# A Fourier token-mixing kernel: the inverse transform's first stage in four quarter tiles of the array, its second in whole-array products

## The chip, the cores and the metric

The kernel runs on one core of a Trainium2 chip. The metric is the time of one execution on the device, in microseconds (us); less is better. In what follows PE is TensorE (the matrix unit, 128 rows by 128 columns), DVE is VectorE, ACT is ScalarE, POOL is GpSimd and SP is SyncE, whose queue issues every DMA of this kernel. PSUM is the memory that PE writes its products into, in banks of 512 float32 a partition.

## The reference, cut to what matters

```python
def _attn_ref(x, filt_r, filt_i):                 # x: 8 x 3136 x 256
    X = np.fft.rfft(x, axis=1)                    # along the 3136 tokens
    Y = X * (filt_r + 1j * filt_i)[None, :, :]
    return np.fft.irfft(Y, n=x.shape[1], axis=1)

def _moe_ref(x, w_ch1, w_ch2):                    # x: what _attn_ref gave
    mixed = np.real(np.fft.fft(np.fft.fft(x, axis=1), axis=2))
    u = x + mixed
    un = (u - mean(u)) / sqrt(var(u) + 1e-6)      # over the 256 channels
    return u + np.maximum(un @ w_ch1, 0.0) @ w_ch2
```

A filter in the frequency domain for each of 8 batches, then a Fourier mixing over tokens and channels (the token part of it is at hand already: it is the filtered spectrum), a normalisation, and a two-layer perceptron with 1024 hidden units.

## The kernel before, in words

All float32 data that goes into PE is split into two float16 parts, high and low, and a product is the sum of three: high by high, high by low, low by high.

**Per batch, the way out** (`there`, lines 598-602). `forward1` (372-405; for batch 0 `first_forward1`, 331-370) loads x in seven tiles of 112 partitions, finds the largest value (`absmax`, on DVE), splits x, multiplies by the 112 x 112 matrix `s1` (line 400: three matmuls of 512 columns for each of 14 pieces), splits the result into `st` on ACT and DVE, and stores it to a scratch array `d1` in DRAM. `forward2` (413-541) loads `d1` back transposed in seven chunks `at` (line 425), and in each chunk does for both halves of the channels: 16 matmuls of 56 columns with the `s2` matrices (`spectrum`, lines 449-450), the filter on DVE and POOL (455-464), the split into `y16`, and a transpose into `z` (for batch 0 on PE, `flip`; for the others by a DMA, line 480). Two chunks later comes the **first inverse stage**, `inverse1` (509-520): two steps a chunk, each of them six matmuls 112 x 112 by 256 columns (lines 514-516: two residues `j`, three products each) into one PSUM bank, the split of the bank into `bt` by ACT (518) and DVE (519), and a store to the scratch array `d2` (520). `fold` (482-507) prepares sums and differences `eo` for the channel mixing.

**Per batch, the way home** (`back`, 604). `inverse2` (543-594) loads `d2` back in seven pieces (554), and in 14 steps does the **second inverse stage**: four matmuls of 512 columns (line 577), in two column tiles of 64 columns of the array: `h` picks the half of the array and of the 128 output partitions, and the two terms of a half, `i`, are accumulated; the high and the low part of the data lie on alternating partitions, so that one pass takes both. ACT scales the bank into `ys` (584), and after each second step four DMAs (five in the first) store `ys` to a scratch array `dy` (560).

**For all tokens** (lines 608-988): groups of 256 slots. `fetch` loads them from `dy`, `prepare` mixes channels (646), normalises and splits into `ut`; `first_product` (six matmuls of 512 columns, line 770) and `second_product` (12 matmuls of 256 columns, line 799) are the perceptron, eight times for each of 49 groups. Their evictions are lines 779 (ACT), 780 and 808 (DVE).

**What sets the order.** The main loop (976-993) goes over the 8 x 49 perceptron pieces. With each, it lets the way out of the next batch go on by some of its steps (`advance`: a batch has `STEPS` = 63 steps, 24 for `forward1`, 4 of pause, 35 for `forward2`: five a chunk, namely `spectrum` twice, `inverse1` twice and `fold`), and the way home by one (`give`: `BACK` = 17 steps a batch). `folds` says at which step a fold would overwrite the ring `eo`; `weigh` places the loading and splitting of the weights at numbered steps during batch 0. Tiles wait for a free buffer of their pool; the PSUM pool `ps_f` of four banks serves both forward stages, both inverse stages and the channel mixing. The order of the instructions on each engine is made by the tile framework from a simulated timeline, by the order of the program, and `after(...)` pins some DMAs and products behind others. All DMAs go through SP's queue in order: one that waits for its data holds up all that stand behind it.

Of the kernel before, what the change touches and what calls it, by code (L numbers as in the profile page):

```python
# [9 lines left out]
F32 = mybir.dt.float32  # L10
# [4 lines left out]
ALU = mybir.AluOpType  # L15
# [23 lines left out]
STEPS = FIRST + PAUSE + 7 * 5  # L39
# [6 lines left out]
LOAD_AT = (19, 20, 21, 22, 50, 50, 54, 54)  # L46
LOAD_AFTER = (("d1", 10), ("d1", 11), ("d1", 12), ("d1", 13), ("bt", 3), ("bt", 3), ("bt", 4), ("bt", 4))
LOAD_IN = ("ut", "ut", "ys", "ys", "big", "big", "big", "big")
WIDEN_AT = (58, 59, 60, 61, 62, 63, 64, 65)
BOUND_AT = (62, 66)  # L50
SPLIT_AT = (63, 115)
# [29 lines left out]
def residue(h, jp):  # L81
    return jp if h == 0 else (28 if jp == 0 else 56 - jp)


# [5 lines left out]

def constants():
    k = slot_freqs()
    n1 = np.arange(112)
    n2 = np.arange(28)
    s1 = np.zeros((112, 56, 2))
    s2 = np.zeros((56, 2, 28, 2, 28))
    for U in range(56):
        j, s = divmod(U, 2)
        th2 = 2 * np.pi * ((n2[:, None] * k[U][None]) % N) / N
        if U == 0:  # L100
            s1[:, 0, 0] = 1
            s1[:, 0, 1] = np.where(n1 % 2, -1, 1)
            lo = n2 < 14
            s2[0, 0, :, 0, :] = np.cos(th2) * lo
            s2[0, 0, :, 1, :] = -np.sin(th2) * lo
            s2[0, 1, :, 0, :] = np.cos(th2) * ~lo
            s2[0, 1, :, 1, :] = -np.sin(th2) * ~lo
            s2[0, 0, :, 1, 0] = np.where(n2 % 2, -1, 1)
        else:
            k1 = 28 if U == 1 else (j if s == 0 else 56 - j)  # L110
            th = 2 * np.pi * ((n1 * k1) % 112) / 112
            s1[:, U, 0] = np.cos(th)
            s1[:, U, 1] = -np.sin(th)
            s2[U, 0, :, 0] = np.cos(th2)
            s2[U, 1, :, 0] = np.sin(th2)
            s2[U, 0, :, 1] = -np.sin(th2)
            s2[U, 1, :, 1] = np.cos(th2)

    p = channel_order()[:129]
# [7 lines left out]

    ncls = np.array([residue(h, jp) for h in range(2) for jp in range(28)])
    i1 = np.zeros((28, 2, 2, 28, 56, 2))
    for j in range(28):  # L130
        for s in range(2):
            for q in range(28):
                U = 2 * j + s
                kk = k[U, q]
                for ri in range(2):
                    if U == 0 and q == 0:
                        con = [(0, 1.0)] if ri == 0 else [(N // 2, 1.0)]
                    elif ri == 0:
                        con = [(kk, 1.0), ((N - kk) % N, 1.0)]
                    else:  # L140
                        con = [(kk, 1j), ((N - kk) % N, -1j)]
                    for tgt, ro in [(j, None)] if j else [(0, 0), (28, 1)]:
                        for kq, cf in con:
                            if kq % 56 != tgt:
                                continue
                            v = cf * np.exp(2j * np.pi * ((ncls * kq) % N) / N) / 32
                            if ro is None:
                                i1[j, ri, s, q, :, 0] += v.real
                                i1[j, ri, s, q, :, 1] += v.imag
                            else:  # L150
                                i1[j, ri, s, q, :, ro] += v.real

    tok = slot_tokens()
    i2 = np.zeros((2, 2, 2, 28, 64))
    j = np.arange(28)
    for jp in range(2):
        for kind in range(2):
            for s in range(2):
                h = s if kind == 0 or jp == 0 else 1 - s
                for q in range(28):  # L160
                    n = tok[kind, 2 * jp + s, q]
# [886 lines left out]
```

## Time and profile before

| | |
|---|---|
| median of three runs | 1534.46 us (1533.2 to 1537.94) |
| the profiled execution: from its first to its last instruction | 1534.0 us |
| busy: PE | 1398.7 us (91%), 11331 matmuls |
| busy: DVE / ACT / POOL | 1092.8 us (71%) / 771.3 us (50%) / 539.9 us (35%) |
| granted TensorE clock, mean | 0.955 |
| DMA | 268.98 MB, 429491 packets, the 16 engines busy for 72.5% of the span |

A row of an instruction group in the profile names the line, the engine and the operation, what is written and read, the shape (partitions x elements), the count, the busy time and the mean duration of one, and the idle time of the engine ahead of it with what ended it. A row of the timeline gives start and length of a run of equal instructions. Matmuls are pipelined: the length of one (385 ns for 512 columns) is longer than the distance to the next, so the cost of a matmul is read from the distances between starts.

### The profile page before, as it was taken

Reading aid. Unit: us, or ns where it says so; the run is one execution under the profiler, and the core shown is the slowest. Engines: PE = TensorE matmul, PEld = TensorE weight load, DVE = VectorE, ACT = ScalarE, POOL = GpSimd, SP = SyncE. Lnnn points to the kernel's source line nnn. Section 1 sums busy time; section 2 is a strip of 40 time slices with the busy share of each in tenths; the row PEclk is TensorE's granted clock in tenths of the full one; section 3 lists DMA queues with packets and bytes.
Section 4 is the critical chain, followed back from the end, with each engine's and each line's share of the span. In section 5 each row is a group of like instructions: output and inputs, shape, how many; then the busy total and the mean of one; then the engine's idle time right before and its main releaser. Section 6 shows DMA issues by size and latency. Waiting matters only on the chain.

```text
span 1534.0 us, 30300 instructions
## 1 busy us (share of the span) xinstructions
PE 1398.7 (91%) x11331; PEld 934.1 (61%) x11331; DVE 1092.8 (71%) x2388; ACT 771.3 (50%) x1426; POOL 539.9 (35%) x682
## 2 busy tenths in 40 slices
PE   5454899787999999999999999899999999999998
PEld 1432567454665677566765677566665667666666
DVE  5576878586967887687758877688767877565562
ACT  4466545354545464474544654374644655443341
POOL 3652049205810195006720284016620284110110
PEclk8675999998999999999999999999999999999999
DMA  8868478959985797859986796859876896644320
GB/s 263 218 205 219 101 163 176 219 157 206 203 216 146 175 227 174 208 152 214 192 192 161 192 231 159 211 146 220 183 189 158 195 237 144 166 107 110 95 55 29
DMA packets 429491, 268.98 MB, mean 175 GB/s; under 512 B 218624, under 2 KB 395824, under 8 KB 429344
## 3 DMA queue, kind: packets, MB, share of 16 engines
q1 hardware_dynamic: 429344, 267.05, 72.5%
q8 instruction: 89, 1.46, 0.4%
q14 instruction: 58, 0.48, 0.1%
HBM read 113.36 MB, written 102.76 MB: 141 GB/s over the span
## 4 chain that ended last, share of the span: by engine, by line
PE 67%; DMA 11%; DVE 7%; issue 3%; POOL 3%; ACT 2%; SPq 1%; DVEq 0%; POOLq 0%; ACTq 0%
PE h L770 26%; PE acc L799 26%; DMA x<-x 3%; PE s L400 3%; PE y L577 3%; DMA at<-d 2%; PE mix L646 2%; DVE y L656 2%; PE i L514 1%; DMA b<-d 1%; PE i L516 1%; PE i L515 1%; PE s L449 1%; DVE mx L267 1%; PE s L450 1%
## 5 line engine op out<-in xcount | busy, mean ns | idle before, releaser
L770 PE MATMUL h<-ut,w1s 128*128 128x512 f16 x2352 | 590.8, 385 | 24.6 <-DVE h L780 20.5
L799 PE MATMUL acc<-w2s,h 128*128 128x256 f16 x4704 | 599.9, 274 | 1.3 <-DVE h L780 1.3
L799 PEld LDWEIGHTS <-h 128*128 128x128 f16 x4704 | 456.4, 98 | 146.8 <-issue 13.6
L779 ACT ACTIVATE h<-h 128x512 f16<-128x512 f32 x392 | 233.1, 595 | 411.9 <-PE h L770 404.6
L780 DVE SCALAR_TENSOR_TENSOR h<-h,h 128x512 f16<-128x512 f32 x392 | 267.6, 683 | 200.3 <-ACT h L779 199.3
L741 POOL TENSOR_TENSOR u<-un,u 128x512 f16<-128x512 f32 x94 | 107.8, 1163 | 758.0 <-ACT u L739 745.6
L770 PEld LDWEIGHTS <-w1s 128*128 128x128 f16 x2352 | 223.8, 99 | 236.7 <-issue 48.1
L656 DVE SCALAR_TENSOR_TENSOR y<-mix,alpha,y 128x508 f32<-128x508 f32 (+1 forms) x368 | 156.0, 474 | 8.2 <-PE mix L646 6.9
L736 ACT ACTIVATE un<-y,sb 128x256 f32<-128x256 f32 x196 | 101.8, 589 | 44.0 <-DVE sb L729 38.8
L469 POOL TENSOR_TENSOR y<-yt,y 128x448 f16<-128x448 f32 x105 | 108.4, 1036 | 16.5 <-ACT y L468 16.2
L584 ACT ACTIVATE ys<-y,alpha 128x512 f32<-128x512 f32 x112 | 76.1, 686 | 71.4 <-PE y L577 71.0
L519 DVE TENSOR_TENSOR bt<-i,bt 112x512 f16<-112x512 f32 x112 | 75.7, 682 | 49.1 <-ACT bt L518 47.4
L267 DVE TENSOR_REDUCE mx<-x 112x1 f32<-112x1024 f32 x56 | 67.7, 1214 | 52.0 <-DMA x<-x 52.0
L463 POOL TENSOR_TENSOR yt<-yt,t 128x224 f32<-128x224 f32 x112 | 73.9, 660 | 81.9 <-DVE t L459 53.6
L455 DVE SCALAR_TENSOR_TENSOR yt<-s,pF,ft 128x448 f32<-128x448 f32 x112 | 75.3, 675 | 37.7 <-PE s L450 34.9
L449 PE MATMUL s<-s,at 112*128 112x56 f16 x896 | 62.7, 191 | 32.6 <-DMA at<-d 28.1
L400 PE MATMUL s<-x,s 112*112 112x512 f16 x294 | 87.3, 388 | 3.9 <-ACT x L394 1.9
L577 PE MATMUL y<-b,i 112*64 112x512 f16 (+1 forms) x480 | 74.1, 396 | 18.1 <-DMA b<-d 17.9
L518 ACT CAST bt<-i 112x512 f16<-112x512 f32 x112 | 64.9, 585 | 49.9 <-PE i L516 43.7
L808 DVE SCALAR_TENSOR_TENSOR y<-acc,beta,y 128x512 f32<-128x512 f32 x98 | 71.2, 742 | 25.7 <-PE acc L799 25.5
L468 ACT CAST y<-yt 128x448 f16<-128x448 f32 x112 | 62.6, 564 | 38.6 <-POOL yt L464 35.6
L449 PEld LDWEIGHTS <-at 112*128 112x128 f16 x896 | 55.8, 98 | 42.6 <-DMA at<-d 36.0
(133 smaller groups left out, 1663.4 us busy)
## 6 DMA issues: line engine op xcount, KB each, us to landing
x<-x SPq DMA_DIRECT2D x56, 448.0 KB
d<-ast SPq DMA_DIRECT2D x112, 224.0 KB
at<-d SPq DMA_DIRECT2D x56, 448.0 KB
d<-bt SPq DMA_DIRECT2D x112, 224.0 KB
b<-d SPq DMA_DIRECT2D x56, 448.0 KB
out<-y SPq DMA_DIRECT2D x98, 256.0 KB
y<-dy SPq DMA_DIRECT2D x92, 256.0 KB
dy<-ys SPq DMA_DIRECT2D x208, 112.0 KB
```

The lines of the kernel that those rows point to most:

```text
L267: nc.vector.tensor_reduce(dst, src, axis=axis, op=ALU.max, apply_absolute_value=True)
L400: nc.tensor.matmul(p, s1[:, hs], x16[:, hx], start=i == 0, stop=i == 2)
L449: nc.tensor.matmul(o, w, s2[:, U, 0].rearrange("p (r k) -> p r k", r=2), start=True, stop=False)
L469: last = half(b, hf == 1).tensor_tensor(ylo, ytv, yhi, op=ALU.subtract)
L577: nc.tensor.matmul(p[64 * h : 64 * h + 64, js], i2[:, t, h, i], bt[:, o + js.start : o + js.stop, h], start=i == 0, stop=i == 1,)
L656: nc.vector.scalar_tensor_tensor(out, p, al, y, op0=ALU.mult, op1=ALU.add)
L736: nc.scalar.activation(un[:m, k], y[:m, t, k], AF.Identity, bias=sb[:m, i, 1:2], scale=sb[:m, i, 3:4])
L741: marks["u16", g] = low.tensor_tensor(u16[:m, :, :, 1], unv, u16[:m, :, :, 0], op=ALU.subtract).ins
L770: marks["pe"] = nc.tensor.matmul(p[:, c0 : c0 + n].rearrange("p (t k q) -> p t k q", k=2, q=m), w1s[:, d, hw, 128 * f : 128 * f + 128], ut ...
L779: nc.scalar.activation(h[:, 0, :nt], p[:, :nt], AF.Relu)
L780: marks["h"] = nc.vector.scalar_tensor_tensor(h[:, 1, :nt], p[:, :nt], 0.0, h[:, 0, :nt], op0=ALU.max, op1=ALU.subtract).ins
L799: nc.tensor.matmul(acc[:m, k], h[:, hh, c0 : c0 + m], w2s[:, f, hw], start=f == 0 and k == 0 and i == 0, stop=f == 7 and k == 1 and i == 2,)
```

## The change

1. **x in slot order.** The host lays the tokens of x out in the order in which the kernel numbers its slots. The first forward matrix `s1` now forms an even and an odd part of each of two token halves: it has 128 output columns (two parts, 56 used of 64 each), and a second version of it for the first token class (`cls`). `st` and `d1` have 128 partitions in place of 112. `s2` is kept for each part `P`; chunk 0 gets extra products with a small matrix `s2x`.
2. **First inverse stage.** `inverse1` is one step a chunk. Both PSUM banks of the chunk are taken at once. The 64 x 64 quarters of the array work on their own products: the row half `h` picks the residue pair and the bank, the column half `P` the part. Six matmuls of 256 columns for each quarter, 24 a chunk (30 in chunk 0, with `i1x`), are issued in turns over the four quarters (`run`), all but the first at high priority. Each bank is scaled and split into `bt` by ACT and DVE as before, and stored by two DMAs in place of one.
3. **Second inverse stage.** Three matmuls of 512 columns over the whole array (`dense`) in place of four in two column tiles; the high and low parts lie side by side in a row of `d2`. Two stores to `dy` for each second step in place of four.
4. **Steps.** `STEPS` is 56: four steps a chunk in `forward2`. The numbered steps for weights and folds are moved along. `at` is loaded by two DMAs, one for each part, in place of one. `bt` and `st` share six buffers in place of four.

The diff, cut to its core:

```diff
-STEPS = FIRST + PAUSE + 7 * 5
+STEPS = FIRST + PAUSE + 7 * 4
...
-    s1 = cp.tile([112, 2, 112], F16, name="s1")
+    s1 = cp.tile([112, 2, 2, 128], F16, name="s1")
+    s2x = cp.tile([112, 2, 2, 56], F16, name="s2x")
-    i1 = cp.tile([112, 28, 2, 112], F16, name="i1")
-    i2 = cp.tile([112, 2, 2, 2, 64], F16, name="i2")
+    i1 = cp.tile([128, 14, 2, 2, 64], F16, name="i1")
+    i1x = cp.tile([64, 2, 2, 64], F16, name="i1x")
+    i2 = cp.tile([112, 2, 2, 128], F16, name="i2")
...
+    def run(todo):
+        for i in range(max(len(m) for m in todo)):
+            for n, m in enumerate(todo):
+                if i < len(m):
+                    o, w, x, start, stop = m[i]
+                    with tc.high_priority() if i + n else nullcontext():
+                        nc.tensor.matmul(o, w, x, start=start, stop=stop)
+
+    def dense(p, w, xs, special):
+        last = None
+        for sl, cls in ((slice(0, 1), 1), (slice(1, 2), 0)) if special else ((slice(0, 2), 0),):
+            terms = [(v, x) for v, x in zip(w(cls), xs)]
+            for i, (v, x) in enumerate(terms):
+                last = nc.tensor.matmul(p[:, sl], v, x[:, sl], start=i == 0, stop=i == len(terms) - 1)
+        return last
...
-            for i, (hs, hx) in enumerate(((0, 0), (0, 1), (1, 0))):
-                nc.tensor.matmul(p, s1[:, hs], x16[:, hx], start=i == 0, stop=i == 2)
-            st = fp.tile([112, 2, 2, 256], F16, tag="ast", name=f"ast_{b}_{q}", bufs=4)
+            dense(p, split_of(s1), [x16[:, i] for i in (0, 1, 0)], q == 0)
+            st = fp.tile([128, 2, 2, 256], F16, tag="ast", name=f"ast_{b}_{q}", bufs=6)
...
-                last = nc.sync.dma_start(ats[ch], d1v[:, 8 * ch : 8 * ch + 8])
+                for P in range(2):
+                    last = nc.sync.dma_start(ats[ch][:, P], d1v[:, P, 4 * ch : 4 * ch + 4])
...
+            for j in range(4):
+                for P in range(2):
+                    o = p[:, P, 56 * j : 56 * j + 56]
+                    of = [(at[:, P, j, 128 * hf : 128 * hf + 128], s2[:, 4 * ch + j, P])]
+                    if ch + j == 0:
+                        of.append((at[:, 1 - P, j, 128 * hf : 128 * hf + 128], s2x[:, 1 - P]))
+                    ms = [(w, m[:, i]) for w, m in of for i in range(2)]
+                    for i, (w, m) in enumerate(ms):
+                        with order if j + P + i == 0 else nullcontext():
+                            nc.tensor.matmul(o, w, m, start=i == 0, stop=i == len(ms) - 1)
...
-        def inverse1(ch, h):
-            z = zs[ch][:112].rearrange("p (j l) c -> p j l c", l=2)[:, 2 * h : 2 * h + 2]
-            j = 4 * ch + 2 * h
-            p = bank(f"i1_{b}_{ch}_{h}")[:112].rearrange("p (j c) -> p j c", j=2)
-            for i in range(2):
-                nc.tensor.matmul(p[:, i], i1[:, j + i, 0], z[:, i, 0], start=True, stop=False)
-                nc.tensor.matmul(p[:, i], i1[:, j + i, 0], z[:, i, 1], start=False, stop=False)
-                nc.tensor.matmul(p[:, i], i1[:, j + i, 1], z[:, i, 0], start=False, stop=True)
-            bt = fp.tile([112, 2, 2, 256], F16, tag="ast", name=f"bt_{b}_{ch}_{h}", bufs=4)
-            nc.scalar.copy(bt[:, :, 0], p)
-            marks["low"] = nc.vector.tensor_tensor(bt[:, :, 1], p, bt[:, :, 0], op=ALU.subtract).ins
-            marks["bt", ch] = nc.sync.dma_start(d2[:, j : j + 2], bt).ins
+        def inverse1(ch):
+            z = zs[ch].rearrange("p (r l i) c -> p r l i c", r=2, l=2)
+            p = [bank(f"i1_{b}_{ch}_{h}").rearrange("p (i c) -> p i c", i=2) for h in range(2)]
+            todo = []
+            for h in range(2):
+                for P in range(2):
+                    rows, mine = slice(64 * h, 64 * h + 56), []
+                    for i in range(2):
+                        ws = i1[rows, 2 * ch + i, P]
+                        ms = [(ws[:, m], z[rows, P, l, i]) for m, l in ((0, 0), (0, 1), (1, 0))]
+                        if ch + h + i == 0:
+                            ms += [(i1x[rows, 1 - P, m], z[rows, 1 - P, l, i]) for m, l in ((0, 0), (0, 1), (1, 0))]
+                        o = p[h][64 * P : 64 * P + 64, i]
+                        mine += [(o, w, x, n == 0, n == len(ms) - 1) for n, (w, x) in enumerate(ms)]
+                    todo.append(mine)
+            run(todo)
+            for h in range(2):
+                bt = fp.tile([128, 2, 2, 256], F16, tag="ast", name=f"bt_{b}_{ch}_{h}", bufs=6)
+                nc.scalar.activation(bt[:, :, 0], p[h], AF.Copy, scale=1.0 / 32)
+                marks["low"] = nc.vector.scalar_tensor_tensor(
+                    bt[:, :, 1], p[h], 1.0 / 32, bt[:, :, 0], op0=ALU.mult, op1=ALU.subtract
+                ).ins
+                for P in range(2):
+                    marks["bt", ch] = nc.sync.dma_start(
+                        d2[:, P, :, 4 * ch + 2 * h : 4 * ch + 2 * h + 2].rearrange("m r j l x -> m r (j l x)"),
+                        bt[64 * P : 64 * P + 56].rearrange("p i l x -> p (i l x)"),
+                    ).ins
...
-                for js, t in parts:
-                    for i in range(2):
-                        for h in range(2):
-                            nc.tensor.matmul(
-                                p[64 * h : 64 * h + 64, js],
-                                i2[:, t, h, i],
-                                bt[:, o + js.start : o + js.stop, h],
-                                start=i == 0,
-                                stop=i == 1,
-                            )
-            nc.scalar.activation(ys[:, o : o + 2], p, AF.Copy, scale=al[:, 2:3])
+                dense(p, split_of(i2), [bt[:, ms, i] for i in (0, 1, 0)], c == 0)
+            nc.scalar.activation(ys[:, ms], p, AF.Copy, scale=al[:, 2:3])
+            if c % 2:
+                for k in range(2):
+                    marks["sp"] = marks["dy"] = nc.sync.dma_start(
+                        dy[k, 224 * (c // 2) : 224 * (c // 2) + 224].rearrange("(j q) c -> q j c", j=4), ys[64 * k : 64 * k + 56]
+                    ).ins
...
-        d1 = dp.tile([112, 28, 2, 256], F16, tag="d1", name=f"d1_{b}")
-        d2s[b] = dp.tile([112, 28, 2, 256], F16, tag="d2", name=f"d2_{b}")
+        d1 = dp.tile([128, 28, 2, 256], F16, tag="d1", name=f"d1_{b}")
+        d2s[b] = dp.tile([28, 2, 2, 28, 2, 256], F16, tag="d2", name=f"d2_{b}")
...
-        "x": c(x.reshape(nb, 112, 28, C)[..., perm]),
+        "x": tokens(x[..., perm]),
```

More of the change, by code (lines that the diff above doesn't have):

```diff
@@ new lines, in hi_lo @@
+def hi_lo(a, axis):
+    return np.stack(split16(a), axis=axis)
+def constants():
+    a1, a2 = transforms()
+    inv = a1.transpose(0, 2, 1, 4, 3).reshape(2, 2, 2, 28, 2, 56).swapaxes(3, 4).reshape(2, 2, 2, 56, 56)
+    q = np.arange(28)
+    at = q // 4 * 4 + q % 2 * 2 + q % 4 // 2
+    inv = inv.reshape(2, 2, 2, 2, 28, 56)[..., at, :].reshape(2, 2, 2, 56, 56) * 4096 / N
+    sign = np.array([[1.0, 1.0], [1.0, -1.0]])
+    s1 = np.zeros((2, 56, 2, 2, 64))
+    i2 = np.zeros((2, 56, 2, 2, 64))
+    for cls in range(2):
+        s1[:, :, cls, :, :56] = np.einsum("kq,qpio->kipo", sign, a1[cls])
+        i2[:, :, cls, :, :56] = np.einsum("kp,qpio->qiko", sign, inv[cls])
+    s1, i2 = (m.reshape(112, 2, 128) for m in (s1, i2))
+    s2 = a2[:, [0, 1], [0, 1]]
+    rows = [np.stack([v, v], axis=-2) for v in (s2, a2[0, [0, 1], [1, 0]])]
+    packed = []
+    for v in rows:
+        h, l = split16(v)
+        l[..., 1, :] = 0
+        v = np.stack([h, l], axis=-2).reshape(v.shape[:-3] + (112, 2, 56))
+        packed.append(np.ascontiguousarray(np.moveaxis(v, -3, 0)))
+    w = np.ones((28, 2, 56))
+    w[0, :, 0] = 0.5
+    back = (a2 * w[:, None, :, None]).transpose(0, 2, 1, 4, 3).reshape(28, 2, 2, 56, 2, 28)
+    back = np.pad(back.swapaxes(4, 5).reshape(28, 2, 2, 56, 56), ((0, 0),) * 4 + ((0, 8),))
+    i1 = np.zeros((2, 64, 14, 2, 64))
+    i1[:, :56] = back[:, [0, 1], [0, 1]].reshape(14, 2, 2, 56, 64).transpose(1, 3, 0, 2, 4)
+    i1x = np.zeros((64, 2, 64))
+    i1x[:56] = back[0, [0, 1], [1, 0]].transpose(1, 0, 2)
@@ L126, in constants @@
     cmix[0, 0, 256:] = 1
[L128 to L151, printed above, removed]
@@ L279, in _program @@
     mixed = [0]
[L280 removed]
+    y16s = [cp.tile([128, 2, 2, 4, 64], F16, name=f"y16_{h}") for h in range(4)]
     for t in y16s:
[L282 removed]
+        nc.gpsimd.memset(t[..., 56:], 0.0)
     sxs, alphas, dys, esps = {}, {}, {}, {}
@@ L430, in load @@
                         load_i1(ch)
+                        if ch == 0:
+                            nc.sync.dma_start(s2x, a["c_s2x"])
+                            nc.sync.dma_start(i1x, a["c_i1x"])
                         if ch == 6:
@@ L914, in give @@
             come[0] += 1
-    folds = {FIRST + PAUSE + (4, 9, 14, 19, 24, 29, 34)[ch]: 224 * ch + 224 for ch in range(7)}
+    folds = {FIRST + PAUSE + (4, 8, 12, 16, 20, 24, 27)[ch]: 224 * ch + 224 for ch in range(7)}
     def need(slot):
```

192 lines of the change are left out of this document (85 added, 107 removed).

## The prediction, made before the changed kernel was built or run

> **What bounds the kernel now.** I read the page first, then the stretches, then single visits of PE to the two stages on the timeline, and last the waits. The page:
>
> ```profile
> span 1534.0 us, 30300 instructions
> PE 1398.7 (91%) x11331; PEld 934.1 (61%) x11331; DVE 1092.8 (71%) x2388; ACT 771.3 (50%) x1426; POOL 539.9 (35%) x682
> PE 67%; DMA 11%; DVE 7%; issue 3%; POOL 3%; ACT 2%; SPq 1%; DVEq 0%; POOLq 0%; ACTq 0%
> ```
>
> PE is the busiest engine and holds two thirds of the chain that ends last. A share over the whole span mixes stages, so the stretches follow (columns: stretch, its length, busy time of PE, weight loads, DVE, ACT, POOL, granted clock, DMA share, GB/s):
>
> ```profile
> 0.00:50.00 50.00, 21.75 (x52) 8.38 (x53) 22.10 (x47) 15.70 (x31) 14.81 (x28) 0.77 0.88 266
> 340.00:370.00 30.00, 18.46 (x165) 9.93 (x165) 21.60 (x57) 15.46 (x30) 11.05 (x14) 0.72 0.86 205
> 370.00:1400.00 1030.00, 1005.22 (x8291) 675.32 (x8289) 766.03 (x1684) 537.56 (x997) 387.16 (x489) 0.99 0.78 184
> 540.00:548.00 8.00, 7.64 (x60) 5.34 (x57) 5.73 (x13) 4.99 (x10) 8.00 (x10) 1.00 1.03 249
> ```
>
> From 370 to 1400 us PE is busy for 1005 of 1030 us at nearly the full clock. There, PE time that is taken away should come off the span. The start is another matter: PE works less than half of the first 50 us, and DMA is at 0.88. Between 340 and 370 us stands one hole, which comes back below. So the question is how many PE slots the change frees in batches 1 to 7, and what new waits it makes.
>
> **The first inverse stage.** Seven chunks in each of batches 1 to 7 are 49 visits. One step of such a visit, six matmuls, and what follows it:
>
> ```profile
> 559.24 0.27 PE L514 MATMUL i<-z,i 112*112 112x256 f16 x1
> ...
> 559.79 0.27 PE L516 MATMUL i<-z,i 112*112 112x256 f16 x1
> 559.90 0.38 PE L770 MATMUL h<-ut,w1s 128*128 128x512 f16 x1
> ```
>
> Six matmuls take 559.90 - 559.24 = 0.66 us, 0.109 us each; a chunk has two steps, 1.31 us. The change has 24 matmuls in four quarters: if four run together, six rounds. Nothing in this trace uses quarter tiles. The nearest rows are a visit to the second inverse stage, which uses two column tiles. Timeline of PE, the second pair of the same visit (from a narrower window), and the weight loads:
>
> ```profile
> 630.51 1.47 PE L799 MATMUL acc<-w2s,h 128*128 128x256 f16 x12
> 631.91 0.62 PE L577 MATMUL y<-b,i 112*64 112x512 f16 x4
> 632.47 1.47 PE L770 MATMUL h<-ut,w1s 128*128 128x512 f16 x6
> 633.77 1.47 PE L799 MATMUL acc<-w2s,h 128*128 128x256 f16 x12
> 635.09 0.38 PE L770 MATMUL h<-ut,w1s 128*128 128x512 f16 x1
> ```
>
> ```profile
> 632.15 0.38 PE L577 MATMUL y<-b,i 112*64 112x512 f16 x2
> ```
>
> ```profile
> 631.91 0.14 PEld L577 LDWEIGHTS <-i 112*64 112x64 f16 x4 [0.21 <-issue]
> 632.47 0.11 PEld L770 LDWEIGHTS <-w1s 128*128 128x128 f16 x2 [0.41 <-issue]
> ```
>
> Reading: 12 matmuls of L799 take 635.09 - 633.77 = 1.32 us when a whole-array product follows, but 631.91 - 630.51 = 1.40 when the tiled visit follows: going in costs 0.08 to 0.09 us. Six matmuls of L770 take 1.30 us, so one of 512 columns takes 0.217. The first pair starts at 631.91, the second at 632.15: two matmuls of 512 columns really ran together, with a lag of 0.023 us. The next product starts 0.32 after the second pair: going out costs 0.10. So a visit pays 0.20 us for changing the array's layout and back (its loads wait too, 0.21 and 0.41 us).
>
> For four quarters a round is at best 0.109 us (one matmul of 256 columns) and with the lag of the pair 0.132. I take 0.12, between two near ends. A visit is then 6 x 0.12 + 0.20 = 0.92 us in place of 1.31, a gain of 0.39; 42 visits gain 16.4 us. Chunk 0 has three extra products in two quarters, nine rounds: 1.28 us, a gain of 0.03, seven times 0.2. Sum: **-16.6 us** (ends -20.1 and -12.8).
>
> Whether weights load while another product runs decides this. In the rows above all four loads of the visit, two of them for the second pair, start within 0.14 us of the first pair, 0.10 us ahead of the second pair's start, and all use the same 112 rows. Against this speaks a sentence in the Trainium skill, "TensorE: Matmul & The Clock Gate", section "Part 3: Packing small matmuls — row/col tiling": a weight load overlaps running matmuls "only when row_grp differs". By it, each round's loads would wait for the round before; this trace disagrees for column tiles. It has a rival of its own below.
>
> **The second inverse stage.** Before: 0.09 + 0.56 = 0.65 us (the rows above). After: three whole-array matmuls, 3 x 0.217 = 0.65 us, with no change of layout. **0 us**; two column tiles plus the change of layout cost what a third product costs. An error of 0.02 us in a visit would be 2 us over 98 visits.
>
> **The s2 products.** Chunk 0 has four more for each half of the channels.
>
> ```profile
> 561.32 0.19 PE L449 MATMUL s<-s,at 112*128 112x56 f16 x1
> ...
> 561.74 0.49 PE L799 MATMUL acc<-w2s,h 128*128 128x256 f16 x3
> ```
>
> Sixteen take 0.42 us, 0.026 each; eight more in seven batches are **+1.5 us**. The first forward stage streams as many columns as before (two classes in one piece make six matmuls of 256 columns in place of three of 512): 0.
>
> **Evictions.** The operations change form, not size:
>
> ```profile
> L780 DVE SCALAR_TENSOR_TENSOR h<-h,h 128x512 f16<-128x512 f32 x392 | 267.6, 683 | 200.3 <-ACT h L779 199.3
> L779 ACT ACTIVATE h<-h 128x512 f16<-128x512 f32 x392 | 233.1, 595 | 411.9 <-PE h L770 404.6
> L519 DVE TENSOR_TENSOR bt<-i,bt 112x512 f16<-112x512 f32 x112 | 75.7, 682 | 49.1 <-ACT bt L518 47.4
> L518 ACT CAST bt<-i 112x512 f16<-112x512 f32 x112 | 64.9, 585 | 49.9 <-PE i L516 43.7
> ```
>
> 683 against 682 ns on DVE, 595 against 585 on ACT, beside engines that are idle for 29% and 50%: 0. Both banks are now taken at once and come free one after the other; the four-bank pool gives them back some 2 x 0.6 + 0.7 us after the last round. PE has perceptron products from other banks to do meanwhile; without that cover it would cost up to 0.6 us a visit.
>
> **SP's queue.** Issues a batch: `bt` +14, `at` +7, `dy` from 30 to 14, so +5. One issue takes 0.3 to 0.4 us (rows below), 2 us of a batch; the second store of a `bt` stands right behind the first, with the same wait. Nothing is moved past another queue. In the steady part 0, hidden beside PE.
>
> **The start (batch 0).** Here waits count, not PE slots. Chain, to the second load of `d2`, and the size of a `d1` store:
>
> ```profile
> 91.93 0.36 PE i L514
> ...
> 94.43 0.23 PE i L516
> 94.72 0.59 ACT bt L518
> ...
> 105.92 0.32 SPq L560
> ...
> 107.17 0.42 SPq L560
> ...
> 107.69 4.23 DMA b<-d
> ```
>
> ```profile
> d<-ast SPq DMA_DIRECT2D x112, 224.0 KB
> ```
>
> The last chunk's 12 products run at half speed, 2.7 us. Six rounds at that speed take some 1.8 us, but now both evictions come behind the last round, +0.6, and a second store, +0.4: 0 together. The four `dy` stores in front of the load of `d2` become two: -0.8. `d1` grows from 112 to 128 rows, 14 x 32 KB = 0.46 MB; at 266 GB/s that is 1.7 us if the transfers bound the first 50 us, and 0 if they are hidden; with DMA at 0.88 I take +1.0. Three more issues (`at`, `s2x`, `i1x`) ahead of the second chunk: +0.8. Sum: **+1 us** (-2 to +4).
>
> **The grid of steps.** After the start, 392 perceptron pieces share some 1360 us, 3.47 us each; 49 of them carry one batch's steps, so a step lasts 2.7 us with 63 of them and 3.0 with 56. `forward1` (28 steps with its pause) is stretched by an eighth: loads of x and `at` get four steps, 12.1 in place of 10.8 us, before they are needed. `forward2` is squeezed: a chunk comes every 12.1 us in place of 13.5. What stalls there now:
>
> ```profile
> PE h L770 <- DVE h L780: 20.5, 12, 4.1
> PE s L449 <- DMA at<-d: 17.6, 10, 10.4
> ```
>
> ```profile
> 358.75 0.23 PE L449 MATMUL s<-s,at 112*128 112x56 f16 x1 [10.37 <-DMA at<-d]
> ```
>
> Ten waits for `at` cost 17.6 us from 175 to 1400 us, one of them 10.4. With 1.3 us more in hand for the first of each batch at most 7 x 1.3 = 9 us go; most waits are shorter, I take **-2 us**. The other end is +9: squeezed chunks meet a DMA system that is already full in a dense stretch (1.03 at 540 to 548 us, above).
>
> **Sum:** -16.6 + 0 + 1.5 + 0 + 1 - 2 = -16.1 us. The profiled execution's 1534.0 us become 1517.9; the median of the runs shown lies 0.5 above it, which gives **1518 us**, with 1510 to 1527 as this case's own range.
>
> **Rivals.** *The hole closes.* The 10.4 us wait also lets the clock fall: from 340 to 370 us PE is granted 0.72, and 18.46 us busy at that clock are 5.2 us lost, so the hole costs about 15.6. If the longer pause closes it: 1518 - 15.6 = 1502 us. For it: the pause; against: 1.3 us doesn't cover 10.4, only another order does. 0.18.
>
> *PE isn't the bound where it matters.* If the chain through DMA and DVE sets the pace of each batch, the freed slots become idle: 1534 us. For it: 20.5 us of waits for DVE's `h`; against: 1005 of 1030 us. 0.08.
>
> *The visits are cut up.* The framework may put whole-array products between the quarters; each cut costs 0.20 us, and two a visit eat the gain: 1534 us. For it: every row above shows stages interleaved; against: the high priority of all but the first matmul. 0.05.
>
> *Squeezed chunks starve PE* (slower). The place is the first load of `at` or a DMA transpose into `z` in `forward2`, the price of one hole 15.6 us with its clock, and it decides from the second new hole on: 1518 + 2 x 15.6 = 1549 us. For it: DMA at 1.03; against: the load of `d2` needs half as many packets, each of 1024 bytes in place of 512. 0.08.
>
> *Loads don't overlap* (slower). A round is then load plus product, about 2 x 0.11 = 0.22 us; a visit 1.52 us, +0.21 x 42 = +8.8, and chunk 0 with nine rounds 2.18, +0.87 x 7 = +6.1; with the other terms 1534.5 + 14.9 + 0.5 = 1550 us. This is what the skill's sentence above would make of the time. The four loads within 0.14 us speak against it. 0.05.
>
> **How the numbers follow.** The forecast has 0.56. Faster by over 0.3% (4.6 us, about what a measurement of this kernel can tell from no change): 0.56 + 0.18 = 0.74. Within: 0.08 + 0.05 = 0.13. Slower: 0.08 + 0.05 = 0.13. The range 1500 to 1534 us takes in the forecast's own range, the closed hole and the lost gain, and leaves out the two slower cases and a little below.
>
> **What would show it.** In the changed kernel's profile: 24 matmuls of a chunk within about 0.9 us and no whole-array product among them; starts of a round's four within a few hundredths and rounds 0.12 apart; the next load waiting about 0.4 us behind a visit; second-stage visits of three matmuls at 0.217 with no idle load; PE's busy share of the middle still at 97%. Rounds 0.2 us apart would prove the loads rival, holes in PE with a clock under 0.9 the squeezed one, and a middle at 95% with the same span the lost gain. The forecast is wrong if the visits cost over 1.2 us or if new holes sum to over 16 us.

## The result, and the profile after

The changed kernel is slower: median 1554.66 us (1551.14 to 1560.1, four runs) against 1533.83 (1530.06 to 1537.94, four runs) for the kernel before; the ratio is 1.0143 with a 95% interval of 1.0114 to 1.0171. The forecast was 1518 us with a range from 1500 to 1534, and 0.13 for slower by over 0.3%. One of the ten executions of e1 below, 2416.6 us at a granted clock of 0.555, was in a slow state and is left out of its ratio.

The same rows of the page, of the changed kernel (its profiled execution spans 1554.1 us):

```profile
span 1554.1 us, 31721 instructions
PE 1397.3 (90%) x12018; PEld 921.9 (59%) x12018; DVE 1088.8 (70%) x2388; ACT 770.1 (50%) x1426; POOL 538.6 (35%) x682
PE 48%; DMA 16%; DVE 15%; POOL 7%; issue 6%; ACT 4%; SPq 3%; DVEq 0%; POOLq 0%; ACTq 0%
```

PE's share of the chain that ends last fell from 67% to 48%, DMA's rose from 11% to 16%, DVE's from 7% to 15%, SP's queue from 1% to 3%. The busy times hardly tell anything: 1397 after 1399. The stretches:

```profile
0.00:50.00 50.00, 22.74 (x108) 11.91 (x108) 26.26 (x56) 16.72 (x33) 17.99 (x33) 0.76 0.95 301
340.00:370.00 30.00, 20.29 (x187) 10.62 (x187) 20.17 (x51) 17.38 (x33) 10.48 (x13) 0.77 0.88 221
370.00:1400.00 1030.00, 978.62 (x8639) 649.31 (x8636) 752.33 (x1661) 524.49 (x979) 386.98 (x489) 0.98 0.76 183
```

The middle is where it went wrong: PE is busy for 979 us of 1030, where it was 1005. The start is not: the first product of the perceptron begins at 147.9 us, before at 147.4. What PE waits for there, from 175 to 1400 us (first the kernel before, then the changed one; us in total, times, longest):

```profile
PE h L770 <- DMA ut<-u: 4.1, 2, 3.2
PE y L577 <- DMA b<-d: 2.7, 3, 1.9
...
PE i L514 <- DMA z<-y: 1.1, 2, 0.7
```

```profile
PE h L798 <- DVE h L808: 17.2, 13, 2.6
PE y L349 <- DMA b<-d: 14.9, 6, 5.2
PE s L481 <- DMA at<-d: 14.0, 14, 2.6
PE h L798 <- DMA ut<-u: 10.7, 2, 8.8
PE i L341 <- DMA z<-y: 9.3, 6, 3.3
PE acc L827 <- DVE y L836: 5.4, 5, 2.7
```

The loads of `d2` cost PE 12 us more than before, the transposes into `z` 8, a late eviction of the accumulators 5; `at` and `ut` together 3 (14.0 + 10.7 after 17.6 + 4.1). The six waits for `d2` stand ahead of the first product of the second inverse stage, in six of the seven batches; of the six for `z`, three stand ahead of a batch's last visit to the first inverse stage and make up 6 of the 9 us. In the trace as a whole, from the 61st matmul of line 770 (798) on, PE's gaps sum to 50 us before and 75 after.

PE's own work in the two stages did nearly what the sum said. A visit to the first inverse stage, its weight loads, and a visit to the second:

```profile
1308.76 1.47 PE L827 MATMUL acc<-w2s,h 128*128 128x256 f16 x12
1310.16 0.85 PE L341 MATMUL i<-z,i 56*64 56x256 f16 x24
1310.94 1.47 PE L798 MATMUL h<-ut,w1s 128*128 128x512 f16 x6
```

```profile
1310.16 0.58 PEld L341 LDWEIGHTS <-i 56*64 56x64 f16 x24 [0.21 <-issue]
1310.94 0.33 PEld L798 LDWEIGHTS <-w1s 128*128 128x128 f16 x3 [0.20 <-issue]
```

```profile
983.55 0.81 PE L349 MATMUL y<-b,i 112*128 112x512 f16 x3
984.20 1.46 PE L798 MATMUL h<-ut,w1s 128*128 128x512 f16 x6
```

24 matmuls in 0.78 us, plus the usual 0.09 for going in (1310.16 - 1308.76 less 12 x 0.109): 0.87, where 0.92 was forecast. All 24 weights were loaded within 0.58 us of the start, while the products ran. The second stage takes 984.20 - 983.55 = 0.65 us, as forecast. SP's queue shows what the sum had not. Its timeline at the end of the last batch, from 4 us ahead of the last first-inverse visit (1317.64 us) to the load of `d2`, comes first; below it the same place in the kernel before, where that visit begins at 1303.78 us:

```profile
1313.59 0.81 SPq L563 DMA_DIRECT2D d<-bt  x1
1314.51 1.26 SPq L511 DMA_TRANSPOSE z<-y  x1
1315.82 5.45 SPq L563 DMA_DIRECT2D d<-bt  x6
1321.38 1.91 SPq L774 DMA_TRANSPOSE ut<-u  x1
1323.34 0.80 SPq L563 DMA_DIRECT2D d<-bt  x1
1324.24 1.26 SPq L774 DMA_TRANSPOSE ut<-u  x1
1325.60 3.27 SPq L563 DMA_DIRECT2D d<-bt  x4
1328.97 0.99 SPq L839 DMA_DIRECT2D out<-y  x2
1330.64 1.00 SPq L600 DMA_DIRECT2D b<-d  x2
```

```profile
1305.14 2.62 SPq L746 DMA_TRANSPOSE ut<-u  x2
1307.85 1.00 SPq L520 DMA_DIRECT2D d<-bt  x2
1308.95 0.94 SPq L811 DMA_DIRECT2D out<-y  x2
1311.26 0.95 SPq L554 DMA_DIRECT2D b<-d  x2
```

Before, the load goes out 7.5 us after the start of the visit, after the change 13.0; this batch is the worst of the seven, and the means follow in a table below. A single `bt` store takes 0.8 us of the queue, and not only here (all stores: shortest/median/longest in ns, before and after):

```profile
L520 SPq DMA_DIRECT2D d<-bt x112: 303/375/1508, 64.4 to 1308.5; - x112
```

```profile
L563 SPq DMA_DIRECT2D d<-bt x224: 758/760/1454, 59.4 to 1328.1; - x112
```

Twice as many stores, each half as large and each twice as long in the queue: their durations sum to 177 us in place of 50. That became the first theory.

### The profile page after: what moved, and what is told of

Read it like the earlier page. It is cut to its first block, busy times and chain, and to the rows that moved or that the text cites. A ratio compares the mean times of both kernels' runs of the same rounds, so it can differ in the third digit from the quotient of the medians.

```text
span 1554.1 us, 31721 instructions
## 1 busy us (share of the span) xinstructions
PE 1397.3 (90%) x12018; PEld 921.9 (59%) x12018; DVE 1088.8 (70%) x2388; ACT 770.1 (50%) x1426; POOL 538.6 (35%) x682
## 3 DMA queue, kind: packets, MB, share of 16 engines
q1 hardware_dynamic: 406816, 270.45, 69.9%
## 4 chain that ended last, share of the span: by engine, by line
PE 48%; DMA 16%; DVE 15%; POOL 7%; issue 6%; ACT 4%; SPq 3%; DVEq 0%; POOLq 0%; ACTq 0%
PE h L798 19%; PE acc L827 18%; DMA x<-x 4%; PE s L349 4%; DVE y L684 3%; PE y L349 3%; DMA d<-ast 2%; DVE h L808 2%; DMA at<-d 2%; PE s L481 2%; PE mix L674 2%; DMA b<-d 2%; DMA out<-y 1%; DVE mx L270 1%; DVE st L741 1%
## 5 line engine op out<-in xcount | busy, mean ns | idle before, releaser
L349 PE MATMUL y<-b,i 112*128 112x512 f16 (+1 forms) x360 | 97.2, 390 | 33.1 <-DMA b<-d 33.1
L494 POOL TENSOR_TENSOR yt<-yt,t 128x224 f32<-128x224 f32 x112 | 74.7, 667 | 119.9 <-DVE t L490 72.5
L559 DVE SCALAR_TENSOR_TENSOR bt<-i,bt 128x512 f16<-128x512 f32 x112 | 73.8, 682 | 54.0 <-ACT bt L558 53.6
L481 PE MATMUL s<-s,at 112*128 112x56 f16 x1792 | 73.0, 194 | 21.7 <-DMA at<-d 18.3
L481 PEld LDWEIGHTS <-at 112*128 112x128 f16 x1856 | 68.7, 100 | 38.2 <-DMA at<-d 25.3
L349 PE MATMUL s<-x,s 112*128 112x512 f16 (+1 forms) x315 | 86.5, 376 | 4.7 <-ACT x L419 3.1
L427 DVE TENSOR_TENSOR ast<-s,ast 128x512 f16<-128x512 f32 x98 | 66.7, 684 | 14.4 <-ACT ast L426 13.1
```

What stands on the lines that cost most here:

```text
L349: last = nc.tensor.matmul(p[:, sl], v, x[:, sl], start=i == 0, stop=i == len(terms) - 1)
L481: nc.tensor.matmul(o, w, m, start=i == 0, stop=i == len(ms) - 1)
```

## The experiments

Two theories: **S**, the stores hold up SP's queue and all that stands in it; **G**, the grid of four steps leaves too little time at the end of a batch, whatever the stores cost. Ratios are to the kernel before on the same chip, with 95% intervals; "us" beside a ratio is the ratio less one, times 1534.

| run | edit | ratio (interval) | us |
|---|---|---|---|
| the changed kernel | | 1.0143 (1.0114 to 1.0171) | +22 |
| e1 | changed, plain store | 1.0036 (1.0009 to 1.0063) | +6 |
| e2 | changed, five steps a chunk | 1.0057 (1.0033 to 1.0082) | +9 |
| e3 | e1 and e2 together | 0.9997 (0.9977 to 1.0017) | 0 |
| e4 | before, slow stores | 1.0047 (1.0022 to 1.0073) | +7 |
| e5 | before, four steps a chunk | 0.9988 (0.9965 to 1.0010) | -2 |
| e6 | e1, no priority for the quarters | 1.0059 (1.0038 to 1.0080) | +9 |
| e7 | e1, one more step ahead of the second stage | 0.9964 (0.9940 to 0.9988) | -6 |
| e8 | before, a third of the first-inverse products left out | 0.9906 (0.9874 to 0.9938) | -14 |
| e9 | before, one more step | 1.0017 (0.9997 to 1.0037) | +3 |
| e10 | e1, two plain stores | 1.0089 (1.0057 to 1.0121) | +14 |
| e11 | e7, two more steps at the tail | 0.9929 (0.9907 to 0.9951) | -11 |
| e12 | changed, one more step | 1.0014 (0.9989 to 1.0038) | +2 |
| e13 | before, slow stores and four steps | 1.0053 (1.0031 to 1.0076) | +8 |
| e14 | before, slow stores and one more step | 1.0049 (1.0022 to 1.0076) | +8 |
| e15 | e13, a third of the products left out | 1.0009 (0.9988 to 1.0030) | +1 |
| e16 | e11 with a second more step | 0.9863 (0.9839 to 0.9886) | -21 |
| e17 | before, two more steps | 0.9920 (0.9894 to 0.9946) | -12 |
| e18 | changed, the steps of e16 | 0.9996 (0.9970 to 1.0022) | -1 |

**The store and the grid, taken back one by one (e1, e2), and put into the kernel before one by one (e4, e5).**

```diff
 e1 (changed kernel)
-                for P in range(2):
-                    marks["bt", ch] = nc.sync.dma_start(
-                        d2[:, P, :, 4 * ch + 2 * h : 4 * ch + 2 * h + 2].rearrange("m r j l x -> m r (j l x)"),
-                        bt[64 * P : 64 * P + 56].rearrange("p i l x -> p (i l x)"),
-                    ).ins
+                marks["bt", ch] = nc.sync.dma_start(d2[:, 4 * ch + 2 * h : 4 * ch + 2 * h + 2], bt).ins
...
-        d2v = d2.rearrange("m p r j l c -> (p r j) m (l c)")
+        d2v = d2.rearrange("(p m r) j l c -> p (r j) m (l c)", p=2, r=2)
...
-        d2s[b] = dp.tile([28, 2, 2, 28, 2, 256], F16, tag="d2", name=f"d2_{b}")
+        d2s[b] = dp.tile([128, 28, 2, 256], F16, tag="d2", name=f"d2_{b}")
 e2 (changed kernel; STEPS and the numbered steps as in the kernel before)
                     f(ch) if arg is None else f(ch, arg)
                     yield
+                    if f is inverse1:
+                        yield
 e4 (kernel before)
-            marks["bt", ch] = nc.sync.dma_start(d2[:, j : j + 2], bt).ins
+            for s in range(2):
+                marks["bt", ch] = nc.sync.dma_start(
+                    d2[28 * s : 28 * s + 28, 0:2, j : j + 2].rearrange("m r j l c -> m r (j l c)"),
+                    bt[56 * s : 56 * s + 56].rearrange("p j l c -> p (j l c)"),
+                ).ins
 e5 (kernel before; STEPS and the numbered steps as in the changed kernel)
-                (c, spectrum, 0), (c, spectrum, 1), (c - 2, inverse1, 0), (c - 2, inverse1, 1),
+                (c, spectrum, 0), (c, spectrum, 1), (c - 2, inverse1, None),
```

> The changed kernel, with the scratch array of the first inverse stage laid out in 128 rows, so that each bt is stored by one DMA of 128 rows of 2048 bytes (as st is) in place of two with 2 x 28 rows; its load is two DMAs in place of one. Theory S (stores): in the changed kernel a bt store holds SP's queue 0.76 us, 224 of them 177 us against 50 before, and everything behind them (loads of d2, transposes, loads of at) comes late. Then the stores here cost about 112 x 0.35 = 39 us of the queue, the waits of PE for d2 and z fall below 8 us together, and the time falls from 1555 to 1515 to 1530 us. Theory G (grid): the shorter tail between the last spectrum and the last first-inverse visit makes PE wait, whatever the stores cost. Then the time stays at 1545 to 1555 us.

> The changed kernel with an empty fifth step behind each first-inverse visit, so that a batch has 63 steps as before. Theory G: from the last spectrum to the last first-inverse visit there are 6 steps again in place of 4, the waits for z and for d2 go, and the time falls to 1515 to 1530 us. Theory S: the stores still hold the queue 0.76 us each, and the time stays at 1545 to 1560 us.

> The kernel before, with each bt store split into two DMAs of 2 x 28 rows of 2048 bytes, the form that the changed kernel has; nothing else differs. Theory S: 224 stores at 0.76 us in the queue, 120 us more of it than before, and the time rises from 1534 to 1550 to 1570 us. Theory G: nothing that counts is changed, 1530 to 1538 us.

> The kernel before, with both halves of a first-inverse chunk in one step, so that a batch has 56 steps and the numbered steps stand as in the changed kernel. Theory G: PE waits for z and d2 at the end of each batch, and the time rises to 1550 to 1570 us. Theory S: 1530 to 1540 us.

The medians: e1 1543.6 us, between the two ranges; e2 1546.3, at the lower edge of S's; e4 1542.4, between the ranges; e5 1534.8, as S had it. Neither theory holds alone. The plain store takes back 1.0143 - 1.0036 = 1.07%, some 16 us, less than S had it. In its trace PE's waits for `d2` fall from 14.9 to 8.8 us, those for `z` from 9.3 to 8.6 alone: 17 us together, where S had them below 8. The fifth step takes back 0.86%, 13 us, though S gave it nothing; but PE's wait for `d2`, which G wanted gone, is 17.0 us there. On the kernel before, the slow stores cost 7 us, below S's range, and four steps cost nothing, which speaks against G. The plain store also brings a load of `d2` in two DMAs in place of one; what that does by itself was not tried. The stores themselves are as S said. In e1, and in e4:

```profile
L562 SPq DMA_DIRECT2D d<-bt x112: 319/389/1744, 61.3 to 1310.3; - x112
```

```profile
L521 SPq DMA_DIRECT2D d<-bt x224: 758/764/1726, 63.2 to 1319.7; - x112
```

So 120 to 130 us more of the queue's time cost 7 us in one kernel and 16 us in the other; whether that difference is real is taken up below.

**Do freed PE slots pay at all (e8), do the two repairs add (e3), does the load of `d2` bind (e7), what does the priority do (e6).** e8 drops line 516 (the low part of the matrix; its time is read as that of a shorter stage). e7 sets `WAIT` to 3, e6 removes `high_priority`.

> The kernel before, with the third of the three products of the first inverse stage (line 516, the low part of the matrix) left out, and nothing else changed: 4 matmuls of 256 columns in place of 6 in a step. It takes 196 x 0.109 = 21 us of PE slots out of batches 1 to 7, about as many as the quarter tiles do, without any other edit. Theory P: PE sets the pace, freed slots come off the span: 1511 to 1518 us. Theory W: the pace of a batch is set by the way through SP's queue, DMA and the evictions; the freed slots turn into waits of PE for z, d2, at or ut: 1526 to 1536 us, with the waits of PE from 175 to 1400 us up by 10 to 20 us.

> The changed kernel with the plain store of the first of these runs and the empty fifth step of the second. If the two costs add (store about 15 us, grid about 10 us by those runs), the time is 1518 to 1530 us, and PE's waits for z and d2 fall below 6 us together. If the fifth step only helped because the stores held the queue (theory S alone), it is that of the plain store, 1536 to 1545 us.

> The changed kernel with the plain store and one more empty step between the first load of d2 and the second inverse stage (18 steps home in place of 17). If the load of d2 at the end of each batch still binds, its 8.8 us of waits go and the time falls by 5 to 9 us against the plain store. If another wait takes its place, the time stays within 4 us of it.

> The changed kernel with the plain store, and the matmuls of the quarter tiles at the same priority as all others. If the priority makes PE stand at z while other work is ready, the waits for z (8.6 us) shrink and the time falls by 4 to 8 us. If the priority keeps the visits whole, whole-array products come between the quarters, a visit costs more than 1.2 us, and the time rises by 10 us or more. If neither, the order hardly changes: within 4 us.

e8 (1520.4 us) gave 14 us for 21 us of slots: between the ranges and nearer to P, with a third lost in new waits (PE's gaps, counted as above, rise from 50 to 57 us). The premise of the forecast was sound in the kernel before. e3 (1536.1 us) lies above the range for a plain sum, at the lower edge of that for S alone, and its interval overlaps that of e1 (PE's waits for `z` and `d2` sum to 12.5 us, not below 6): that the two repairs add is not shown. e7 (1528.0 us) is by its ratio 11 us below e1, somewhat over the 5 to 9 of a load that binds. Its trace doesn't bear that cause out: the wait for `d2` should have gone and fell by 2 us (e1, then e7):

```profile
PE y L349 <- DMA b<-d: 8.8, 5, 2.1
```

```profile
PE y L349 <- DMA b<-d: 6.7, 3, 2.8
```

`WAIT` also counts in `BACK` and in `need` and `soon`, which pace the whole way home, so the run changes more than this one distance. e6 lies 3.5 us above e1 with overlapping intervals: the third of its expectations. Its visits stand in 60 pieces on the timeline, after 55 in e1.

**Controls and the tail (e9 to e12).** e10 stores each `bt` in two plain halves of 64 rows. e11 adds, to e7:

```diff
         for c in range(9):
+            if c >= 7:
+                yield
             work = [
```

> Control: the kernel before with the third empty step between the first load of d2 and the second inverse stage, nothing else. PE's wait for d2 is 2.7 us there from 175 to 1400 us, so at most 3 us can come off: 1531 to 1537 us. If it is 1527 us or less, the gain that this step gave the plain-store kernel has nothing to do with the change.

> The plain-store kernel with each bt stored by two DMAs of 64 plain rows in place of one of 128: as many stores as the changed kernel, in the plain form. If the form (2 x 28 rows) made a store hold the queue 0.76 us, a store takes 0.3 to 0.4 us here, 224 of them some 80 us of the queue, and the time is that of the plain store within 5 us. If the number counts, or a store of half the rows costs 0.76 us in any form, the queue is held some 170 us and the time is that of the changed kernel, about 1550 us.

> The plain-store kernel with the third empty step on the way home, and one empty step ahead of each of the last two first-inverse visits of a batch (58 steps). If the short tail makes PE wait for z (7.1 us there), that wait falls below 3 us and the time is 1519 to 1526 us. If another wait takes its place: 1526 to 1532 us.

> The changed kernel as it is (slow stores) with the third empty step on the way home. If the slow stores cost time mainly through the load of d2 at the end of each batch (14.9 us of PE's waits), the step covers it: 1535 to 1543 us. If they cost it everywhere, by holding up all that stands in the queue: 1543 to 1552 us.

One more step does nothing for the kernel before (e9), takes 11 us off the plain-store kernel (e7) and 20 us off the changed one (e12, 1.0143 to 1.0014). e12 lies in the range for a step that covers the load of `d2`, but PE's wait for it only falls from 14.9 to 11.3 us, and the 9 us between the two gains have an interval of some 8 on each side: that the step covers the slow stores is not shown. e11 is inside its range at 1521 us, and PE's wait for `z` is gone from its list; its interval overlaps that of e7, so the tail steps by themselves are not shown to pay. In e10 a store of 64 plain rows took longer than one of 128, which fits neither of the two expectations:

```profile
L563 SPq DMA_DIRECT2D d<-bt x224: 445/587/2007, 60.5 to 1319.3; - x112
```

224 stores sum to 136 us of the queue, between the 52 of e1 and the 177 of the changed kernel, and the time lies between theirs. Number and form both count for the queue.

**What was still open (e13 to e18).** e13 and e15 combine the edits of e4, e5 and e8; e14 is e4 with `WAIT` at 3; e16 is e11 with `WAIT` at 4; e17 is the kernel before with `WAIT` at 4; e18 is the changed kernel with the steps of e16.

> The kernel before with both of the edits that were tried on it alone: two stores of 2 x 28 rows for each bt, and four steps a chunk. Alone they gave +0.5% and -0.1%. If they add: 1537 to 1545 us. If the short tail only costs once the stores are slow: 1548 to 1560 us.

> The kernel before with the slow stores and the third empty step on the way home. If the stores cost through the load of d2 at the end of each batch, the step covers it: 1532 to 1538 us. If they cost by holding up the whole queue: 1540 to 1546 us.

> The kernel before with the slow stores, four steps a chunk, and the third product of the first inverse stage left out (21 us of PE slots freed). If freed slots pay as they did alone (14 us): that much below the run with both edits and all products. If the queue and the tail set the pace once the stores are slow, the freed slots turn into waits: within 5 us of that run.

> The kernel with the plain store and the two empty steps ahead of the last first-inverse visits, with a fourth empty step on the way home. If the load of d2 still binds there (6.9 us of waits, three times), 1514 to 1519 us; if the third step was enough, 1519 to 1526 us.

> Control for the best version: the kernel before with a fourth empty step on the way home and nothing else. If the steps on the way home pay by themselves, 1515 to 1528 us; if they only mend what the change broke, 1531 to 1540 us.

> The changed kernel with its slow stores, the fourth empty step on the way home and the two empty steps ahead of the last first-inverse visits: the best version but for the stores. If the steps alone mend the change, because they give the slow stores time to pass, 1514 to 1522 us. If the stores still hold up the queue in the rest of a batch: 1525 to 1540 us.

In the kernel before, store and grid add within the intervals (e13), and a step doesn't cover the stores (e14 lies in the range for a queue held up as a whole). With both edits in, the 21 us of freed slots pay 0.44%, 7 us, where they paid 14 alone (e15, between its two expectations, with intervals of 0.2% on each side); PE's gaps rise by 11 us, from 59 to 70, so part of the freed slots turned into waits. e18 against e16 differs only in the store and load of `d2`: 1.33%, 20 us, although the steps are there, and PE waits no longer for `d2` in e18 (3.4 us) than in e16 (5.7). So in the changed kernel, too, the stores cost outside the end of a batch. e16 is the best version: 1514.38 us, 1.4% below the kernel before, at the lower edge of the range for a load that still binds. But e17 lies in the range for steps that pay by themselves: they give the kernel before 0.8% without any change. At equal `WAIT`, the change with the plain store is worth 0.9920 - 0.9863 = 0.6%, 9 us, and e16 has the two steps at the tail besides, which the kernel before was not given. The step of e17 doesn't pay at `d2`, where PE waits for 3.1 us after 2.7; what falls against e9 (first) is the wait for DVE's `h`, and why was not tried:

```profile
PE h L770 <- DVE h L780: 18.9, 12, 5.0
```

```profile
PE h L770 <- DVE h L780: 9.6, 14, 2.4
```

PE's waits in e16, from 175 to 1400 us:

```profile
PE h L797 <- DVE h L807: 12.7, 15, 2.3
PE h L797 <- DMA ut<-u: 11.2, 2, 11.0
PE s L481 <- DMA at<-d: 9.6, 13, 2.6
PE y L349 <- DMA b<-d: 5.7, 3, 3.1
```

The wait for `z` is no longer on the list, that for `d2` is down from 14.9 to 5.7 us.

Seven pairs of these runs differ only in the layout, store and load of `d2`, and together they say what the slow stores cost. The difference of the ratios in a pair is uncertain by 0.3 to 0.4%, some 4 to 6 us. The last two columns are PE's gaps in the profiled executions, from the 61st product of the perceptron on.

| plain, slow | ratio | us | gaps, plain | gaps, slow |
|---|---|---|---|---|
| before, e4 | +0.47% | 7 | 50.1 us | 61.6 us |
| e5, e13 (before, four steps) | +0.65% | 10 | 50.0 | 59.1 |
| e9, e14 (before, one more step) | +0.32% | 5 | 52.6 | 58.0 |
| e1, changed | +1.07% | 16 | 64.4 | 75.1 |
| e3, e2 (changed, five steps) | +0.60% | 9 | 63.7 | 72.4 |
| e7, e12 (changed, one more step) | +0.50% | 8 | 57.4 | 67.4 |
| e16, e18 (changed, most steps) | +1.33% | 20 | 49.4 | 59.6 |

The slow stores cost in every pair, though with e9 and e14 no more than the uncertainty, and PE's gaps grow by 5 to 12 us, much alike in both kernels. PE's slots without the gaps grow too, by 1 to 2 us in four pairs and by 7 to 8 where the profiled execution with the slow stores had a clearly lower granted clock (e1 to changed 0.955 to 0.946, e16 to e18 0.956 to 0.952, e9 to e14 0.955 to 0.949). The ratios give 13 us in the mean for the changed kernel and 7 for the one before, but the gaps don't show it waiting more for the stores; whether gaps bring the lower clock was not tried.

A table from the traces makes the end of a batch visible, as means over batches 1 to 7. First column: from the start of the last `s2` product to the start of the last first-inverse product. Second: from there to the issue of the last `bt` store. Third: from the issue of the first load of `d2` to the first product of the second stage.

| | last spectrum to last visit | visit to last store | load to second stage |
|---|---|---|---|
| before | 18.2 us | 2.9 us | 5.1 us |
| e4 (before, slow stores) | 18.4 | 5.0 | 4.9 |
| e5 (before, four steps) | 14.1 | 2.9 | 5.1 |
| changed | 14.1 | 7.0 | 4.5 |
| e1 (plain store) | 13.8 | 4.7 | 5.5 |
| e16 (plain store, more steps) | 17.4 | 4.1 | 9.4 |

The slow stores lengthen the second column by 2.1 us on the kernel before and by 2.3 us on the changed one. The changed kernel has another 1.8 us there with the plain store. I put that down to the evictions: both stand behind the last round of 24 products, where the first half's used to run beside the second half's products. The traces bear this out in part: the second eviction ends 2.5 us behind the last product in the kernel before and 3.9 in e1, as means over the seven batches. But in three of them ACT starts the first eviction 2.6 to 3.7 us behind the round, with normalisation work (`un`) in front of it, so the order on ACT counts too. No run tried this by itself.

## Why the prediction was wrong, point by point

- **First inverse stage (-16.6 us): nearly right.** A whole visit cost 0.87 us in place of the 0.92 taken (30 of 37; the rest up to 1.14, with the quarters out of step), chunk 0 some 1.19 in place of 1.28. But five of the 49 visits were cut into two halves that take 0.77 us each, since two of the quarters then stand idle, as in this stretch of the changed kernel:

```profile
958.86 0.84 PE L341 MATMUL i<-z,i 56*64 56x256 f16 x12
959.63 1.04 PE L798 MATMUL h<-ut,w1s 128*128 128x512 f16 x4
960.60 0.84 PE L341 MATMUL i<-z,i 56*64 56x256 f16 x12
```

  In sum 46.0 us with the way out, plus 54 entries of 0.09: 51 us in place of 65, a gain of 14.
- **Loads beside running products: right.** In the visit shown above the second round of four starts 0.134 us behind the first, the later ones 0.109 us apart, the four of a round within 0.014 us. What the Trainium skill says in "TensorE: Matmul & The Clock Gate", "Part 3: Packing small matmuls — row/col tiling", that loads overlap only when the row group differs, taken by itself, does not hold here: each row half has two column quarters with products in flight, and the 24 loads are through in 0.58 us. The kernel before had shown as much for the whole array, which would have priced this rival lower: twelve products of line 799 pass in 1.32 us, 0.109 us each, and each has a load of its own:

```profile
L799 PEld LDWEIGHTS <-h 128*128 128x128 f16 x4704 | 456.4, 98 | 146.8 <-issue 13.6 <-DVE h L780 1.5 <-ACT h L779 0.6
```

- **Second inverse stage (0) and s2 products (+1.5): right.** 0.65 us a visit; the s2 slots rose by 2.3 us.
- **Evictions (0): right in length** (592 and 681 ns medians in the trace), but not in place: the second half's eviction ends 1.1 us later than before at the end of a batch (1.4 in e1).
- **SP's queue (0): this is the step that failed.** "One issue takes 0.3 to 0.4 us, 2 us of a batch ... In the steady part 0, hidden beside PE." I took the issue time of a `bt` store of one shape from rows of stores of other shapes. Measured: 0.76 us, 28 a batch: in sum 22 us of the queue in place of 6 (177 and 50 us over eight batches; all issues in the queue sum to 824 us after 712). And it was not hidden: taken back in place (e1), it is worth 16 us, and PE's gaps shrink from 75 to 64 us. In the other pairs of the changed kernel it is worth 9, 8 and 20 us.
- **The start (+1): right**, +0.5 us to the first perceptron product.
- **The grid of steps (-2): wrong.** Without the one long wait (10.4 us of the 17.6 before, none of the 14.0 after), the waits for `at` rose from 7 to 14 us. And I looked at the loads at the beginning of `forward2` and not at its end, where the four-step grid takes 4 us (18.2 to 14.1) from the transposes into `z`; those waits rose by 8 us. On the kernel before four steps cost nothing (e5). In the changed kernel a fifth step takes back 13 us (e2), with the plain store 6 (e1 to e3, with an interval of 5 on each side).
- **The hole did not close; it changed its name.** Between 330 and 370 us every kernel has one wait of 7.2 to 12.1 us: for `at` in those with five steps a chunk, for `ut` in those with four. In the changed kernel it is 8.8 us. Its cause was not tried.
- **The rivals.** "Squeezed chunks starve PE" (0.08, 1549 us) comes near in time, as does "loads don't overlap" (0.05, 1550 us), which the visits refute. The first named one right place, the transposes into `z`; its mechanism, two or more new holes of 15.6 us, was wrong: it was many waits of up to 5 us, and DMA was not full (69.9% of the span in place of 72.5%). "PE isn't the bound" is refuted for the kernel before by e8. Of the signs named beforehand, new holes of over 16 us in sum came true.

The sum as measured: PE's slots without gaps fell by 5 us from the 61st product on (by 13 in e1, at the clock of the kernel before; 0.946 was granted to the changed kernel, 0.955 to the other two), gaps rose by 25, the start by 0.5; together the 20 us between the two spans. Against the forecast's terms that is 10 us too little from the slots (-5 in place of -15) and 27 too much from waits (+25 in place of -2), which with the start makes up the 36 us between 1517.9 and 1554.1. The plain store takes back 16 us, store and fifth step together 22 (e3). What stays open is the rest: with both taken back the kernel is level with the one before, and the gain of 16 us is still missing. Gaps stay at 64 us in e3 after 50 before, and no run takes that difference apart. Nor is it settled why a second more step on the way home speeds up the kernel before when a first one does nothing.

## What to carry to other kernels

When an edit splits or reshapes a DMA, price its issue from rows of the same shape, or bound it from both sides, and sum it over the one queue that all DMAs share; a queue that is half idle on average is not idle where the next stage's load stands in it. A faster stage in a schedule of fixed steps also takes time away from the transfers between the steps: list, for each transfer, how many steps lie between issue and use before and after, at the end of each batch too. And a change that loses can be right in its core: here the first inverse stage came out 14 us shorter for 16.6 forecast, and two lines that store the result cost 8 to 20 us, by the pair of kernels in which they are compared.

## What the runs showed of the hardware

- Four quarter tiles of 64 x 64 really run at once: 24 matmuls of 256 columns in 0.78 us against 24 x 0.109 = 2.6 us one after the other, with 0.09 us for going into the layout (changed kernel, at 1310.16 us).
- A DMA's issue time in SP's queue went with its shape and not with its bytes: a store of 128 rows of 2048 bytes took 0.32 us at the least and 0.39 in the median (e1), of 64 such rows 0.45 and 0.59 (e10), of 56 rows that go to 28 x 2 rows in DRAM 0.76 and 0.76 (changed kernel).
